# S4 convolution beside a feed-forward block: order of pieces in a spectral visit, six visits for the last inverse step, and a later third bank

## The chip, the core and the metric

The kernel runs on one core of a Trainium2 chip. Its engines run side by side, each through its own list of instructions in order: TensorE (PE, matmuls, with weight loads shown apart as PEld), VectorE (DVE), ScalarE (ACT), GpSimd (POOL) and SyncE (SP, which here only issues transfers). They wait for each other through semaphores. Matmuls write to PSUM, eight banks of 128 partitions x 512 fp32 values; DVE and ACT read the results from there. The metric is the device time of one execution in microseconds, as the median of the runs. In the profile every matmul of fp32 data in small tiles is recorded as two passes; the counts below are of the program's matmuls, unless "recorded" is said.

## The reference

```python
def _A_ref(u, A_re, A_im, B_re, B_im, C_re, C_im, log_dt, Dskip):   # S4 convolution
    dt = jnp.exp(log_dt)[:, None]
    logdA = dt * (A_re + 1j * A_im)
    P = jnp.exp(logdA[:, :, None] * l[None, None, :])               # D x N x L
    K = jnp.einsum("dn,dnl,dn->dl", Cc, P, dt * Bc).real            # kernel of 2048 taps
    y = irfft(rfft(u, 2L) * rfft(K, 2L))[:L] + u * Dskip
    return y
def _B_ref(x, w1, w2):
    return silu(x @ w1) @ w2
xn = layernorm(x)
return x + _A_ref(xn, ...) + _B_ref(xn, w1, w2)
```

(The transform lines are shortened.) L is 2048 tokens, D 576 channels, N 128 states, the hidden width F 4608. All is fp32.

## The kernel before, in words

**The feed-forward block (FFN) is the main stream of PE.** Tokens are worked in halves and blocks of 512, the hidden width in chunks of four tiles of 128. `up()` makes one hidden tile: 14 matmuls of 512 columns into the bank `ph` (lines 343 to 345; each fp32 operand is split into a high and a low part, and three of the four products are kept), then ACT makes `gf` (silu) and its high part `gh`, DVE the low part `gl`. `down()` makes one token tile and half of the channels: a group of twelve matmuls of 288 columns into a bank `po` (line 369), which DVE adds to the accumulator `acc` (line 373). Weights come by DMA and are split by ACT and DVE (`w1h`, `w1l`, `w2h`, `w2l`).

**Banks for `po`.** `banks_of()` (line 114) hands a bank to each group when the program writes it: two banks `ps2` in turn, and every third group the bank `ps3`, whenever `ps3` exists. `ps3` exists while the convolution kernel is generated, not during the spectral stage, and again from the end of that stage (0.876 of the FFN's steps) on. The new `ps3` lies where the spectral stage had its banks.

**The convolution is woven in.** `weave()` steps the FFN generator and moves the generator `side()` on when the FFN has come to a given share of its steps. `side()` first generates the kernel taps, then spreads the input; from 0.601 to 0.876 runs `spectral()`, then `tail()`.

`spectral()` works through 16 pairs of frequencies, each with three kinds of data of 576 columns: the taps `kw` (kind 0), the input `u` (kind 1) and the product `ysw` (kind 2, the first step of the inverse). They are laid end to end and cut into **visits** of up to 1024 columns. `visit()` takes the tile `pf` (pool `psb`, four banks, one buffer: the next visit starts when the banks are evacuated) and issues the visit's pieces, sorted by kind and by descending pair (line 808). A piece is a run of columns of one kind and pair within a bank; it is eight matmuls of 64 x 32 tiles of the array (line 815), which stand side by side in the array. Then ACT and DVE evacuate the pieces in the order in which the visit lists them: `ka` and `ut` by ACT (line 833), `e` by ACT and `yo` by DVE (line 827). DVE makes the products `kb` and `ut` (lines 840 to 844) and the taps `kw` (lines 799 and 801) beside it.

`tail()` does the **last step of the inverse**. `add_conv(j, dsts)` takes four banks `py` (three of `pss`, one of `ps3`) and issues sixteen matmuls of 64 x 32 tiles and 288 columns for the token tiles j and j + 1 (line 947), each bank holding one half of the channels of one tile; DVE adds the four banks to the rows' sums (line 955). There are eight calls: four in `tail()` for tiles 0 to 7, whose sums come back from DRAM as `r0`, and four in `down()` of the last chunk, for tiles 8 to 15, whose sums are still in `acc`.

**What sets the order.** The program's text gives a first order; a scheduler then places the instructions of each engine by its own costs. `high_priority()` moves an instruction up, `behind(x)` forbids it ahead of x. So one moved visit shifts the FFN matmuls around it.

Of the kernel before, what the change touches and what calls it, by code (L numbers as in the profile page):

```python
# [26 lines left out]
HD = D // 2  # L27
# [5 lines left out]
def weave(main, steps, side):  # L33

    at = next(side, None)
    for i, _ in enumerate(main):
        while at is not None and at * steps <= i + 1:
            at = next(side, None)
    while at is not None:
        at = next(side, None)  # L40


@with_exitstack
def kernel(
# [22 lines left out]
    nc = tc.nc  # L67
# [24 lines left out]
    f1 = vt = None  # L92
    s4 = None
# [14 lines left out]
    ps1 = ctx.enter_context(tc.tile_pool(name="ps1", bufs=2, space=PSUM))  # L108
    ps2 = ctx.enter_context(tc.tile_pool(name="ps2", bufs=2, space=PSUM))
    pss = psb = ps3 = None  # L110

    acc = {}

    def banks_of():

        n = 0
        while True:
            n += 1
            pool, tag = (ps3, "ps3") if ps3 and n % 3 == 0 else (ps2, "ps2")
            yield pool.tile([P, 512], F32, tag=tag, name="po")  # L120

    spare = banks_of()

    def new_xt(blk):
# [25 lines left out]
    pins = {}  # L150

    def behind(ins):
        return tc.issue_after(ins) if ins is not None else nullcontext()
# [113 lines left out]
    def ffn():  # L267
# [88 lines left out]
        def down(blk, jj):  # L356
            half, c, b = blk
            j = 8 * half + 4 * b + jj
            js = slice(jj * P, (jj + 1) * P)
            if half == 1 and c == NCH - 1:  # L360
                if jj % 2 == 0:
                    add_conv(j, (acc[j], acc[j + 1]))
            for h in range(2):
                hs = slice(h * HD, (h + 1) * HD)
                po = next(spare)
                n = 0
                for t in range(FT):
                    for g, w in ((0, 0), (0, 1), (1, 0)):
                        pins["pe"] = nc.tensor.matmul(po[:, :HD], G[blk, t][g][:, js], W2[half, c, t][w][:, hs],  # L369
                                                      start=n == 0, stop=n == 3 * FT - 1).ins  # L370
                        n += 1
                with tc.high_priority():
                    nc.vector.tensor_add(acc[j][:, hs], po[:, :HD], acc[j][:, hs])  # L373
# [47 lines left out]
        for i, blk in enumerate(blocks):  # L421
            half, c, b = blk
# [23 lines left out]
            for step in ("u0", "d0", "d1", "d2", "d3", "u1", "u2", "u3"):  # L446
                k = int(step[1])
# [12 lines left out]
    kl = kfp = yp = pa = tail_at = None  # L460
# [293 lines left out]
    def spectral():  # L754
# [49 lines left out]
        def visit(v):  # L804

            banks = psb.tile([P, 2, 2, 512], F32, tag="psb", name="pf")
            last = pins["pe"]
            for kind, p, c, n, b, at in sorted(visits[v], key=lambda piece: (piece[0], -piece[1])):
                for g in (1, 0):
                    gs = slice(64 * g, 64 * g + 64)  # L810
                    for o in (1, 0, 3, 2):
                        os = slice(32 * o, 32 * o + 32)
                        src = (ks[p][gs, 1 - o % 2] if kind == 0 else us[p][gs, o % 2] if kind == 1 else ys[p][gs, o // 2])
                        with tc.high_priority(), behind(last):
                            last = nc.tensor.matmul(banks[os, g, b, at:at + n], mats[p, kind // 2][gs, os], src[:, c:c + n],  # L815
                                                    start=True, stop=True, tile_position=(64 * g, 32 * o),
                                                    skip_group_check=True).ins
            pins["pe"] = last
            for kind, p, c, n, b, at in visits[v]:
                if kind == 2:  # L820
                    if c == 0:
                        yos[p] = kl.tile([P, 2, D], F32, tag="yo", name="yo", bufs=1)
                    e = kl.tile([P, 512], F32, tag="e", name="e", bufs=1)[:, :n]
                    with tc.high_priority():
                        nc.scalar.copy(e, banks[:, 0, b, at:at + n])
                        for h, op in enumerate((ALU.add, ALU.subtract)):
                            pins["turned"] = nc.vector.tensor_tensor(yos[p][:, h, c:c + n], e, banks[:, 1, b, at:at + n], op=op).ins
# [68 lines left out]

    def tail():

        r0s = {}

        def load_r0(j):
            r0s[j] = yp.tile([P, 2, D], F32, tag="r0", name="r0", bufs=4)
            nc.sync.dma_start(r0s[j], dr0[j * P:(j + 2) * P, :].rearrange("(i p) d -> p i d", p=P))

        yield tail_at[0]
        with behind(pins["load"]):
            for j in (0, None, 2, None, None, None, None, None):
                conv_load()
                if j is not None:
                    load_r0(j)  # L910
        for j in range(0, 8, 2):
            if j == 2:
                load_r0(4)
                load_r0(6)
            yield tail_at[1 + j // 4] + j // 2 % 2 * tail_at[3]
            add_conv(j, (r0s[j][:, 0, :], r0s[j][:, 1, :]))
            store(r0s[j], j, (nc.gpsimd,))

    yss = {}

# [14 lines left out]
                nc.sync.dma_start(yss[j][64 * h:64 * h + 64],  # L935
                                  d2.rearrange("(q j r) d -> j r q d", q=4, j=NJ)[j, :, :, h * HD:(h + 1) * HD])

    def add_conv(j, dsts):

        py = [pool.tile([P, 512], F32, tag=t, name="py") for pool, t in ((pss, "pss"),) * 3 + ((ps3, "ps3"),)]  # L940
        first = pins["pe"]
        for n in range(16):
            i, q1, q2, h = 1 - n // 8, n // 4 % 2, n // 2 % 2, 1 - n % 2
            o = 64 * q1 + 32 * q2
            rows = slice(64 * h, 64 * h + 64)
            with tc.high_priority() if n else nullcontext(), behind(first):
                mm = nc.tensor.matmul(py[2 * i + h][o:o + 32, :HD], s4[rows, q2], yss[j + i][rows, 2 * q2 + q1],  # L947
                                      start=True, stop=True, tile_position=(64 * h, o), skip_group_check=True)
            if n == 0:
                first = mm.ins  # L950
        for i in range(2):
            del yss[j + i]
            for h in range(2):
                hs = slice(h * HD, (h + 1) * HD)
                nc.vector.tensor_add(dsts[i][:, hs], py[2 * i + h][:, :HD], dsts[i][:, hs])
        for _ in range(2):
            conv_load()

    def gate_of(i):
# [7 lines left out]
        return t + min(max(t - turn, 0) * lost / (0.5 - turn - lost), lost)  # L967

    def side():
        nonlocal s4, kl, kfp, yp, pa, tail_at, f1, vt, pss, psb, ps3  # L970
        marks = (0.13, 0.601, 0.876)
        tail_at = (0.91, 0.934, 0.967, 0.0072)
        with tc.tile_pool(name="kf", bufs=1) as kfp, tc.tile_pool(name="pss", bufs=3, space=PSUM) as pss, tc.tile_pool(name="ps3", bufs=1, space=PSUM) as ps3:
            for n in ("f", "phi"):
                kf[n] = kfp.tile([P, D], F32, name=n + "T")
            f1 = ident
            vt = kfp.tile([P, 69], F32, name="vt")
# [70 lines left out]
    sd = side()  # L1048
# [97 lines left out]
```

## Time and profile before

| | |
|---|---|
| median of 3 runs | 1092.29 us (1092.09 to 1092.8) |
| profiled execution | 1091.44 us |
| its span | 1089.7 us |
| PE busy | 1080.4 us, 99% |
| DVE busy | 892.1 us, 82% |
| ACT busy | 588.7 us, 54% |
| granted clock of PE | 1.000 |

How to read the rows that follow. A row of the timeline gives the start, the busy time, the engine, the line, the operation, what is written from what, the shape and how many stand in the row; in brackets the time for which the engine was idle before it, and what ended that. PE's matmuls overlap each other in the pipeline, so the spacing of their starts is what one costs, not its busy time. A row of the list of waits gives who waited for whom, the time in all, how often, and the longest. A row of the table by windows gives the window, its length, and for PE and PEld the busy time with the number of recorded instructions, then the clock, the share of DMA and what it moved. A piece of the chain has start, length and what it was.

### The profile page before, as it was taken

What the parts mean: (1) busy time and instruction counts of PE and PEld (TensorE: products, weight loads), DVE (VectorE), ACT (ScalarE), POOL (GpSimd) and SP (SyncE); (2) the same over time, 40 slices, a digit from 0 to 9 for tenths busy, and PEclk for the clock granted to TensorE, in tenths of its full rate; (3) what the DMA queues carried; (4) which work ended last, traced back from release to release, by engine and by line L of the source; (5) the groups of instructions that cost most, each with busy time, mean ns of one, the idle gap of its engine ahead of it and who ended that gap; (6) DMA issues with size and microseconds to landing.
All of it is one profiled execution on the core that took longest, in us unless ns stands there. A gap on an engine that the chain in (4) does not pass through costs nothing.

```text
span 1089.7 us, 24623 instructions
## 1 busy us (share of the span) xinstructions
PE 1080.4 (99%) x10127; PEld 946.9 (87%) x10127; DVE 892.1 (82%) x1463; ACT 588.7 (54%) x934; POOL 138.4 (13%) x241
## 2 busy tenths in 40 slices
PE   9999999999999999999999999999999999999998
PEld 7999998998998999989999898887788787888886
DVE  7799899999999999999999963678888878753443
ACT  4574455767676777676766753435454534432210
POOL 1100000000000000010000004234242432000111
PEclk9999999999999999999999999999999999999999
DMA  9745521342525243427644257558675865438953
GB/s 271 208 125 155 146 67 40 93 113 65 131 70 134 73 102 101 110 82 211 197 133 111 58 119 198 155 152 256 176 226 169 237 179 162 122 99 208 245 159 88
DMA packets 175424, 156.58 MB, mean 144 GB/s; under 512 B 113312, under 2 KB 144800, under 8 KB 175184
## 3 DMA queue, kind: packets, MB, share of 16 engines
q1 hardware_dynamic: 159616, 103.21, 36.8%
q0 software_dynamic: 14944, 50.94, 15.5%
q8 instruction: 79, 1.29, 0.5%
q10 hardware_dynamic: 752, 0.85, 0.3%
q14 instruction: 33, 0.27, 0.1%
HBM read 101.00 MB, written 44.61 MB: 134 GB/s over the span
## 4 chain that ended last, share of the span: by engine, by line
PE 90%; DVE 7%; ACT 1%; issue 1%; DMA 0%; POOL 0%; ACTq 0%; DVEq 0%
PE po L369 40%; PE ph L343 33%; PE pf L815 4%; PE ph L345 3%; PE kp L736 3%; PE ph L344 3%; PE z L663 2%; PE py L947 1%; DVE acc L373 1%; PE pu L171 1%; PE pu L172 1%; DVE gl L354 1%; DVE th L649 1%; DVE S L715 0%; DVE C L704 0%
## 5 line engine op out<-in xcount | busy, mean ns | idle before, releaser
L369 PE MATMUL po<-w2h,gh 128*128 128x288 f32 x1152 | 338.8, 297 | 0.6 <-DVE acc L373 0.6
L369 PE MATMUL po<-w2l,gh 128*128 128x288 f32 x1152 | 339.1, 296 | 0.3 <-DVE w2l L328 0.3
L369 PE MATMUL po<-w2h,gl 128*128 128x288 f32 x1152 | 335.8, 296 | 0.0
L369 PEld LDWEIGHTS po<-w2h,gh 128*128 128x128 f32 x1152 | 215.4, 188 | 16.6 <-issue 6.3
L369 PEld LDWEIGHTS po<-w2l,gh 128*128 128x128 f32 x1152 | 215.8, 188 | 10.4 <-issue 3.8
L369 PEld LDWEIGHTS po<-w2h,gl 128*128 128x128 f32 x1152 | 214.9, 188 | 3.9 <-issue 2.8
L373 DVE TENSOR_TENSOR acc<-po,acc 128x288 f32<-128x288 f32 x288 | 126.2, 452 | 65.9 <-PE po L369 64.8
L351 ACT ACTIVATE gf<-ph 128x512 f32<-128x512 f32 (+1 forms) x146 | 85.3, 587 | 167.2 <-PE ph L345 145.6
L343 PE MATMUL ph<-xh,w1l 128*128 128x512 f32 (+1 forms) x584 | 158.4, 386 | 0.0
L343 PE MATMUL ph<-xh,w1h 128*128 128x512 f32 (+1 forms) x584 | 158.3, 387 | 0.0
L343 PE MATMUL ph<-xl,w1h 128*128 128x512 f32 (+1 forms) x584 | 158.0, 386 | 0.0
L354 DVE TENSOR_TENSOR gl<-gf,gh 128x512 fp32r<-128x512 f32 (+1 forms) x148 | 98.3, 671 | 37.2 <-ACT gh L352 36.3
L343 PEld LDWEIGHTS ph<-xl,w1h 128*128 128x128 f32 x584 | 107.2, 188 | 20.7
L343 PEld LDWEIGHTS ph<-xh,w1l 128*128 128x128 f32 x584 | 107.3, 188 | 20.3
L343 PEld LDWEIGHTS ph<-xh,w1h 128*128 128x128 f32 x584 | 104.0, 188 | 16.8 <-ACT x L143 0.5
L352 ACT CAST gh<-gf 128x512 fp32r<-128x512 f32 (+1 forms) x148 | 89.0, 610 | 51.7 <-PE po L369 49.1
L174 POOL DMA_DIRECT2D d1u<-u x32 | 17.4, 545 | 478.1 <-ACT u L173 478.1
L693 ACT ACTIVATE c<-th,magic 128x1040 f32<-128x1040 f32 x36 | 42.0, 1168 | 39.8 <-DVE C L716 32.0
L695 ACT ACTIVATE c<-th 128x1040 f32<-128x1040 f32 x36 | 38.7, 1075 | 45.6 <-DVE th L694 45.1
L305 DVE TENSOR_TENSOR w1l<-w1r,w1h 128x640 fp32r<-128x640 f32 x72 | 56.5, 818 | 0.2
L345 PE MATMUL ph<-x,w1l 128*128 128x512 f32 (+1 forms) x146 | 56.6, 388 | 0.0
L344 PE MATMUL ph<-x,w1h 128*128 128x512 f32 (+1 forms) x146 | 56.2, 385 | 0.0
(189 smaller groups left out, 1609.7 us busy)
## 6 DMA issues: line engine op xcount, KB each, us to landing
w2r<-in_B_w_dram SPq DMA_DIRECT2D x72, 288.0 KB, 3.7
w1r<-in_B_w_dram SPq DMA_DIRECT2D x35, 512.0 KB, 3.9
d1u<-u POOLq DMA_DIRECT2D x32, 288.0 KB, 2.6
d1k<-stage SPq DMA_DIRECT2D x36, 256.0 KB, 4.7
u<-d1u POOLq DMA_DIRECT2D x16, 576.0 KB, 5.0
kw<-d1k POOLq DMA_DIRECT2D x16, 576.0 KB, 6.0
ysw<-ut SPq DMA_DIRECT2D x64, 144.0 KB, 2.7
d<-yo POOLq DMA_DIRECT2D x32, 288.0 KB, 4.0
```

The lines of the kernel that those rows point to most:

```text
L305: pins["w1l"] = nc.vector.tensor_sub(l1, src, h1).ins
L343: nc.tensor.matmul(ph, w[:, kt, :], v[:, kt, a:e], start=n + kt == 0, stop=False)
L344: nc.tensor.matmul(ph, h1[:, 4, :], x4[:, a:e], start=False, stop=False)
L345: pins["pe"] = nc.tensor.matmul(ph, l1[:, 4, :], x4[:, a:e], start=False, stop=True).ins
L351: nc.scalar.activation(gf, ph, AF.Silu)
L352: pins["gh"] = nc.scalar.copy(gh, gf).ins
L354: pins["gl"] = nc.vector.tensor_sub(gl, gf, gh).ins
L369: pins["pe"] = nc.tensor.matmul(po[:, :HD], G[blk, t][g][:, js], W2[half, c, t][w][:, hs], start=n == 0, stop=n == 3 * FT - 1).ins
L373: nc.vector.tensor_add(acc[j][:, hs], po[:, :HD], acc[j][:, hs])
L693: nc.scalar.activation(c65, th, AF.Identity, bias=magic)
L695: nc.scalar.activation(c65, th, AF.Abs)
L815: last = nc.tensor.matmul(banks[os, g, b, at:at + n], mats[p, kind // 2][gs, os], src[:, c:c + n], start=True, stop=True, tile_position=(6 ...
```

## The change

**Pieces.** A new function `ends_small()` orders the pieces of a visit: of up to three pieces the shortest goes to the front, or stays last if it stood last in the old order; of more than three the two shortest go to the two ends, the one that came earlier in the old order to the front. The rest stay in the old order. Both `visit()` and `add_conv()` use it.

**Last inverse step.** `add_conv(js, dsts)` takes a list of two or three token tiles. With three, the tiles are laid end to end over two banks for each half of the channels: pieces of 288, 224, 64 and 288 columns, each of eight matmuls and two adds. `tail()` does (0, 1, 2), (3, 8, 9), (10, 11, 4) and (5, 6, 7), at 0.934, 0.945, 0.956 and 0.967 of the FFN's steps; `down()` does (12, 13) and (14, 15). The program has 32 matmuls and eight DVE adds more than before. Results of the tiles 0 to 7 are stored once both tiles of a pair are done.

**Third bank.** A flag `third` says whether every third group of `po` goes to `ps3`. It is set at the start of the convolution, cleared before the spectral stage, and set again in `tail()` at 0.91 of the FFN's steps.

```diff
+def ends_small(pieces, key):
+    short = sorted(sorted(pieces, key=lambda piece: piece[3])[:2 if len(pieces) > 3 else 1], key=key)
+    rest = sorted((piece for piece in pieces if piece not in short), key=key)
+    if len(short) == 1 and short[0] == max(pieces, key=key):
+        return rest + short
+    return short[:1] + rest + short[1:]
...
-            pool, tag = (ps3, "ps3") if ps3 and n % 3 == 0 else (ps2, "ps2")
+            pool, tag = (ps3, "ps3") if third and n % 3 == 0 else (ps2, "ps2")
...
             if half == 1 and c == NCH - 1:
-                if jj % 2 == 0:
-                    add_conv(j, (acc[j], acc[j + 1]))
+                if b == 1 and jj % 2 == 0:
+                    add_conv((j, j + 1), acc)
...
-            for kind, p, c, n, b, at in sorted(visits[v], key=lambda piece: (piece[0], -piece[1])):
+            for kind, p, c, n, b, at in ends_small(visits[v], lambda piece: (piece[0], -piece[1])):
...
         yield tail_at[0]
+        third = True
...
-        for j in range(0, 8, 2):
-            if j == 2:
+        for k, js in enumerate(((0, 1, 2), (3, 8, 9), (10, 11, 4), (5, 6, 7))):
+            if k == 1:
                 load_r0(4)
                 load_r0(6)
-            yield tail_at[1 + j // 4] + j // 2 % 2 * tail_at[3]
-            add_conv(j, (r0s[j][:, 0, :], r0s[j][:, 1, :]))
-            store(r0s[j], j, (nc.gpsimd,))
+            yield tail_at[1 + k]
+            add_conv(js, {j: r0s[j - j % 2][:, j % 2, :] if j < 8 else acc[j] for j in js})
+            for j in js:
+                if j < 8 and j % 2:
+                    store(r0s[j - 1], j - 1, (nc.gpsimd,))
...
-    def add_conv(j, dsts):
+    def add_conv(js, dsts):
         py = [pool.tile([P, 512], F32, tag=t, name="py") for pool, t in ((pss, "pss"),) * 3 + ((ps3, "ps3"),)]
...
+        for i, j in enumerate(js):
+            c, at = 0, (512 if len(js) < 3 else HD) * i
+            while c < HD:
+                n = min(HD - c, 512 - (at + c) % 512)
+                pieces.append((i, j, c, n, (at + c) // 512, (at + c) % 512))
+                c += n
...
-        tail_at = (0.91, 0.934, 0.967, 0.0072)
+        tail_at = (0.91,0.934,0.945,0.956,0.967)
...
+            third = True
...
-        ps3 = None
+        third = False
```

**In the order of PE, a pair of visits in the spectral stage** (at 737 us of the profile before). `pf_9005` and `pf_9118` are two visits that follow each other; the second has four pieces. Before, its start and what is around it:

```order
L369 MATMUL po_9345<-w2h_9188,gh_9214 128x288
L815 MATMUL pf_9118<-kw_8767,m2_8765 32x384 x8
L815 MATMUL pf_9118<-u_8763,m2_8609 32x448 x8
L815 MATMUL pf_9118<-u_8763,m2_8609 32x128 x8
L815 MATMUL pf_9118<-ysw_8785,m2_8400 32x64 x8
L369 MATMUL po_9345<-w2l_9189,gh_9214 128x288
```

After:

```order
L379 MATMUL po_9359<-w2h_9188,gh_9214 128x288
L825 MATMUL pf_9118<-u_8763,m2_8609 32x128 x8
L825 MATMUL pf_9118<-kw_8767,m2_8765 32x384 x8
L825 MATMUL pf_9118<-u_8763,m2_8609 32x448 x8
L825 MATMUL pf_9118<-ysw_8785,m2_8400 32x64 x8
L379 MATMUL po_9345<-w2l_9189,gh_9214 128x288
```

The piece of 128 columns has gone to the front. Between the two visits stand 25 FFN matmuls before, 3 of them with 512 columns, and 36 after, 18 of them with 512.

**PE again, at the groups of `po` after the spectral stage** (at 988 us of the profile before). The groups are numbered in the order in which they are handed banks: 12048, 12062, 12076, 12090, 12104, 12118, 12132, 12146. Before, every third of them (12062, 12104, 12146) has the third bank:

```order
L369 MATMUL po_12104<-w2h_11594,gh_11997 128x288
L369 MATMUL po_12104<-w2l_11595,gh_11997 128x288
L369 MATMUL po_12104<-w2h_11594,gl_11998 128x288
L369 MATMUL po_12146<-w2h_11333,gh_11635 128x288
L369 MATMUL po_12146<-w2l_11334,gh_11635 128x288
```

After:

```order
L379 MATMUL po_12132<-w2h_11594,gh_11997 128x288
L379 MATMUL po_12132<-w2l_11595,gh_11997 128x288
L379 MATMUL po_12132<-w2h_11594,gl_11998 128x288
L379 MATMUL po_12146<-w2h_11333,gh_11635 128x288
L379 MATMUL po_12146<-w2l_11334,gh_11635 128x288
```

Before, the two groups that stand side by side have the same bank. After, all of these groups alternate between the two banks of `ps2`, and the group ahead of 12146 has the other bank.

**PE, in the last inverse step** (at 1070 us of the profile before): two calls of `add_conv` with banks `py_12998` to `py_13001` and `py_13089` to `py_13092`. Before:

```order
L947 MATMUL py_12999<-ys_12664,ident_69 32x288
L947 MATMUL py_12998<-ys_12664,ident_69 32x288
L947 MATMUL py_13092<-ys_12825,ident_69 32x288 x4
L947 MATMUL py_13091<-ys_12825,ident_69 32x288 x4
L947 MATMUL py_13090<-ys_12822,ident_69 32x288 x4
```

After, the end of the first of the two calls of two tiles:

```order
L970 MATMUL py_13122<-ys_12738,ident_69 32x288
L970 MATMUL py_13121<-ys_12738,ident_69 32x288 x2
L379 MATMUL po_13145<-w2h_12798,gh_13116 128x288
L379 MATMUL po_13145<-w2l_12799,gh_13116 128x288
L379 MATMUL po_13145<-w2h_12798,gl_13117 128x288
```

Before, two calls follow each other without an FFN matmul between them; after, 42 FFN matmuls stand between this call and the next.

More of the change, by code (lines that the diff above doesn't have):

```diff
@@ L897, in tail @@
     def tail():
+        nonlocal third
         r0s = {}
@@ L936, in conv_load @@
                                   d2.rearrange("(q j r) d -> j r q d", q=4, j=NJ)[j, :, :, h * HD:(h + 1) * HD])
-    def add_conv(j, dsts):
+    def add_conv(js, dsts):
         py = [pool.tile([P, 512], F32, tag=t, name="py") for pool, t in ((pss, "pss"),) * 3 + ((ps3, "ps3"),)]
[L941 to L952, printed above, removed]
+        pieces = []
+        for i, j in enumerate(js):
[4 more added lines that the diff above has]
+                c += n
+        first = last = pins["pe"]
+        for _, j, c, n, b, at in ends_small([(i, j, c, n, b, at) for i, j, c, n, b, at in pieces], lambda piece: -piece[4]):
+            for q in range(4):
+                for h in (1, 0):
+                    q1, q2 = q // 2, q % 2
+                    o = 64 * q1 + 32 * q2
+                    rows = slice(64 * h, 64 * h + 64)
+                    with nullcontext() if first is last else tc.high_priority(), behind(first):
+                        mm = nc.tensor.matmul(py[2 * b + h][o:o + 32, at:at + n], s4[rows, q2], yss[j][rows, 2 * q2 + q1, c:c + n],
+                                              start=True, stop=True, tile_position=(64 * h, o), skip_group_check=True)
+                    if first is last:
+                        first = mm.ins
+        for _, j, c, n, b, at in pieces:
+            yss.pop(j, None)
@@ L953, in add_conv @@
             for h in range(2):
-                hs = slice(h * HD, (h + 1) * HD)
-                nc.vector.tensor_add(dsts[i][:, hs], py[2 * i + h][:, :HD], dsts[i][:, hs])
-        for _ in range(2):
+                d = dsts[j][:, h * HD + c:h * HD + c + n]
+                nc.vector.tensor_add(d, py[2 * b + h][:, at:at + n], d)
+        for _ in js:
             conv_load()
@@ L969, in side @@
     def side():
-        nonlocal s4, kl, kfp, yp, pa, tail_at, f1, vt, pss, psb, ps3
+        nonlocal third, s4, kl, kfp, yp, pa, tail_at, f1, vt, pss, psb, ps3
         marks = (0.13, 0.601, 0.876)
-        tail_at = (0.91, 0.934, 0.967, 0.0072)
+        tail_at = (0.91,0.934,0.945,0.956,0.967)
         with tc.tile_pool(name="kf", bufs=1) as kfp, tc.tile_pool(name="pss", bufs=3, space=PSUM) as pss, tc.tile_pool(name="ps3", bufs=1, space=PSUM) as ps3:
+            third = True
             for n in ("f", "phi"):
@@ L1037, in side @@
         nc.gpsimd.dma_start(s4, cs4)
-        ps3 = None
+        third = False
         with tc.tile_pool(name="kl", bufs=2) as kl, tc.tile_pool(name="psb", bufs=1, space=PSUM) as psb:
```

## The prediction

> **What bounds the kernel now.** I read the page first, then the list of waits of the matrix engine, then its timeline around each wait, then the chain through those places, and last the busy time of single visits.
>
> ```profile
> span 1089.7 us, 24623 instructions
> PE 1080.4 (99%) x10127; PEld 946.9 (87%) x10127; DVE 892.1 (82%) x1463; ACT 588.7 (54%) x934; POOL 138.4 (13%) x241
> PE 90%; DVE 7%; ACT 1%; issue 1%; DMA 0%; POOL 0%; ACTq 0%; DVEq 0%
> ```
>
> The matrix engine (PE) is busy 99% of the span and is 90% of the chain that ended last. So a microsecond is won or lost only where PE stands still, or where its matmuls take longer than the same columns take elsewhere. The profiled execution took 1091.44 us, its span is 1089.7, and it stands 0.85 below the median of 1092.29; I make the sum against 1091.44 and add 0.85 at the end. 0.2% of the median, about what a measurement of this kernel can tell from no change, is 2.18 us: the bounds are 1090.1 and 1094.5.
>
> The list of PE's waits from 676 us on has four rows:
>
> ```profile
> PE py L947 <- DVE r L955: 0.6, 1, 0.6
> PE po L369 <- DVE acc L373: 0.6, 1, 0.6
> PE pf L815 <- issue: 0.4, 1, 0.4
> PE po L369 <- DVE w2l L328: 0.3, 1, 0.3
> ```
>
> Each is a single event, 1.9 us in all, and all of them lie in the stretch that the change rewrites. The holes around them are larger than the list says, because it counts only time in which no matmul is running, and after each stop the pipeline has to fill again. So I measure from start to start.
>
> **The change part by part. (a) The wait of a visit at 737 us.** PE's timeline and three pieces of the chain before it:
>
> ```profile
> 736.61 0.29 PE L369 MATMUL po<-w2h,gh 128*128 128x288 f32 x1
> 737.36 0.88 PE L815 MATMUL pf<-kw,m 64*32 64x384 f32 x16 [0.45 <-issue]
> ...
> 739.52 0.29 PE L369 MATMUL po<-w2h,gl 128*128 128x288 f32 x1
> 739.66 0.29 PE L369 MATMUL po<-w2h,gh 128*128 128x288 f32 x1
> 740.22 0.40 PE L369 MATMUL po<-w2l,gh 128*128 128x288 f32 x1 [0.27 <-DVE w2l L328]
> 740.45 0.30 PE L369 MATMUL po<-w2h,gl 128*128 128x288 f32 x1
> 740.59 0.29 PE L369 MATMUL po<-w2h,gh 128*128 128x288 f32 x1
> 740.88 0.40 PE L369 MATMUL po<-w2l,gh 128*128 128x288 f32 x1
> ```
> ```profile
> 726.60 0.46 DVE acc L373
> ...
> 736.57 0.39 DVE yo L827
> ...
> 739.49 0.68 DVE w2l L328
> ```
> For comparison an undisturbed visit:
> ```profile
> 860.51 0.29 PE L369 MATMUL po<-w2h,gh 128*128 128x288 f32 x1
> 860.73 1.20 PE L815 MATMUL pf<-kw,m 64*32 64x64 f32 x32
> ...
> 862.62 0.40 PE L369 MATMUL po<-w2l,gh 128*128 128x288 f32 x1
> ```
>
> Undisturbed, a visit starts 0.22 us after the FFN matmul ahead of it (860.51 to 860.73), and an FFN matmul of 288 columns follows the last one after 0.14 (739.52 to 739.66). At 737 the visit starts 0.75 after: 0.53 lost. 739.66 to 740.22 is 0.56, so 0.42 lost, and 740.59 to 740.88 0.29, so 0.15. After each of these two stops the next start comes 0.23 instead of 0.14 later (740.22 to 740.45): 0.2 together. The sum is 1.3 us. The cause is one: from 726.60, when PE delivers the sum `po_9076`, VectorE (DVE) works without a pause until 740.17 (739.49 plus 0.68), and the evacuation `yo` of the visit before, which the visit needs because the four banks exist once, is in that row at 736.57, and `w2l` behind it.
>
> In the new order 36 FFN matmuls stand between the two visits in place of 25, and 18 of them are 512 wide in place of 3. DVE has the same nineteen operations between `po_9076`'s sum and the second `w2l` in both orders, so they still take 13.6 us (726.60 to 740.17). The eleven more matmuls alone, at 0.14 each, give PE 1.5 us more work before it needs either result, against 0.53 that are lacking at the visit and 0.42 more at `w2l`. These matmuls are no extra work; PE does them later in the order of before. So (a) is worth -1.3; bounds: -1.3 if all goes, -0.5 if only the visit's own wait goes, since 1.5 less 0.95 leaves a cover of only half a microsecond.
>
> **(b) The third bank at 988 us.**
>
> ```profile
> 987.83 0.29 PE L369 MATMUL po<-w2h,gl 128*128 128x288 f32 x1
> 988.68 0.40 PE L369 MATMUL po<-w2h,gh 128*128 128x288 f32 x1 [0.55 <-DVE acc L373]
> ...
> 990.25 0.29 PE L369 MATMUL po<-w2h,gl 128*128 128x288 f32 x1
> 990.49 0.99 PE L369 MATMUL po<-w2h,gh 128*128 128x288 f32 x3
> 991.32 0.30 PE L369 MATMUL po<-w2l,gh 128*128 128x288 f32 x1
> ...
> 991.59 0.29 PE L369 MATMUL po<-w2h,gh 128*128 128x288 f32 x1
> 991.82 0.40 PE L369 MATMUL po<-w2l,gh 128*128 128x288 f32 x1
> ```
>
> `po_12104` ends at 987.83 and `po_12146` follows directly; both were handed the third bank, so the second waits for the whole chain matmul, `acc` add, matmul. By starts: 987.83 to 988.68 is 0.85, 0.71 too much; the restart 0.09, as at 740.22; then the stop has delayed the release of the buffers of `gh`, and 990.25 to 990.49 loses 0.10, 990.49 to 991.32 (three matmuls, due 0.42) loses 0.41, 991.59 to 991.82 and the restart behind it 0.09 each. Sum 1.5 us. With the third bank handed out from 0.91 on only, these groups alternate between two banks, with twelve matmuls of another group between a bank's end and its next use: 12 x 0.14 = 1.7 us against the 0.85 that bank and add took here. What is late next is the first use of the third bank, `po_12372`; it stands well behind the last evacuation. I take -1.5; bounds -1.5 and 0 (the holes at 990 to 992 come back in another place if `gh` has another holder).
>
> **(c) The order of pieces in a visit.** Busy time of PE in visits of 1024 columns, the last row of two answers of the table by windows: nine visits in which a short piece stands behind a long one with another behind it, and the seventeen others.
>
> ```profile
> sum 25.90, PE 18.72 PEld 9.18; mean PE 2.08 PEld 1.02
> ```
> ```profile
> sum 50.10, PE 33.23 PEld 15.05; mean PE 1.95 PEld 0.89
> ```
>
> All have the same columns; nine of them cost 18.72 - 9 x 1.95 = 1.2 us more. The visit at 860.73 has its 64 columns first and takes 1.89 from its start to the next FFN matmul, so a short piece at the front costs nothing; others of the seventeen have it last. The new rule puts the short ones there in every visit, so I take -1.1 (1.2 less 0.1 for pieces that the scheduler may still mix). Bounds: -1.2, and +0.4 if visits now undisturbed become like the mean of the nine in three cases (3 x 0.13). The loads of `u` and `kw` that change places in the queues of GpSimd and SP cost nothing: no DMA is in the list of waits; their cover is the second buffer of each of these tiles, and without it a late load would show as a wait of `pf`, at a price like that of (a).
>
> The rule also makes one visit fall apart: its piece `u` of 256 columns is issued eleven FFN matmuls ahead of the rest. **A visit's fixed cost** comes from two sizes. The first add_conv:
>
> ```profile
> 1012.74 1.23 PE L947 MATMUL py<-ys,ident 64*32 64x288 f32 x32
> 1013.90 0.41 PE L369 MATMUL po<-w2h,gh 128*128 128x288 f32 x1
> ```
>
> 576 columns take 1.16, 1024 take 1.89: (1.89 - 1.16) / 448 = 1.63 ns a column and 0.22 fixed. Around it lie 0.22 - 0.14 ahead and 0.23 - 0.14 behind, so 0.39 us for each further visit. The split costs +0.4.
>
> **(d) The last step of the inverse.** Eight calls of two tiles become four of three tiles and two of two. Two of the eight stand side by side today:
>
> ```profile
> 1070.55 1.22 PE L947 MATMUL py<-ys,ident 64*32 64x288 f32 x32
> 1072.34 1.78 PE L947 MATMUL py<-ys,ident 64*32 64x288 f32 x32 [0.57 <-DVE r L955]
> 1074.06 0.40 PE L369 MATMUL po<-w2h,gh 128*128 128x288 f32 x1
> ```
> ```profile
> 1071.83 1.55 DVE L955 TENSOR_TENSOR r<-py,r 128x288 f32<-128x288 f32 x4 [2.92 <-PE py L947]
> ```
>
> This pair takes 3.51, where 2 x 1.16 would do: its second half waits for the banks and then goes at the pace of DVE's adds. Before: 6 x 1.16 + 3.51 + 7 x 0.17 around them = 11.7. After: a visit of three tiles has 864 columns, 1.16 + 288 x 1.63 ns = 1.63; 4 x 1.63 + 2 x 1.16 + 6 x 0.17 = 9.9. That is -1.8; the pair stands 42 FFN matmuls apart now. But in the new order the pieces of a three-tile visit stand mixed, and by the nine visits above that costs 0.13 each at most places: I allow 0.1 x 4, so -1.4. Bounds -1.8, and -0.4 (0.22 each, as the dearest of the nine, and one wait of 0.57 for a bank). The 32 more matmuls are in the columns already: a visit of 1024 columns costs the same in 32 recorded passes as in 64.
>
> ```profile
> 730.50:733.40 2.90, 1.95 (x32) 0.49 (x32) 1.00 0.02 6
> ...
> 788.40:791.40 3.00, 1.96 (x64) 1.11 (x64) 1.00 1.06 255
> ```
>
> Against this stands a rule of the Trainium skill, "TensorEngine Tiling (Array Packing)", section Instruction Overhead: each matmul has an overhead of about 60 cycles, so one should not cut a dimension that is small already. If that came on top, eight more matmuls a visit, side by side on eight tiles, would be two passes of 60 cycles; at 0.8 ns a column and pass (half of 1.63) I estimate 0.1 us a visit, 0.4 in all, and the sum would be 0.4 higher. The two rows above speak for nothing on top.
>
>  The eight more adds (by 1.55 / 4 = 0.39 each, 3 us) lie beside PE's work; without that cover they are the second rival. The stores of tiles 4 to 7 move behind the last call; they leave well ahead of the last rows, which are unchanged.
>
> **The sum.** -1.3 - 1.5 - 1.1 + 0.4 - 1.4 = -4.9. For waits that a new order of some 3000 matmuls makes where the trace of before can show none I add +0.4, one wait like that at 740.22. -4.5 on 1091.44 gives 1086.9, and with 0.85, 1087.8 as the median.
>
> **The rivals.** First, the waits move and do not go. (a) and (b) are lateness of DVE and of `gh`, and an order that saves PE 1 us brings it 1 us earlier to the next late result. Against it: outside these places no DVE wait is in the list, and between them PE is the late one. Then -1.1 + 0.4 - 1.4 is left, -2.1: 1090.2, within 0.2%.
>
> Second, DVE paces the three-tile visits. Each leaves eight adds, 3.1 us by the row of 1071.83, and the four banks exist once; between the second and the third such visit stand only 18 FFN matmuls of 512 columns, 0.23 us each by these two rows, 4.2 us:
>
> ```profile
> 1029.73 1.09 PE L343 MATMUL ph<-xh,w1h 128*128 128x512 f32 x4
> 1030.66 1.08 PE L343 MATMUL ph<-xl,w1h 128*128 128x512 f32 x4
> ```
>
> If a `gl` (0.69 in the chain) and two other adds come between, the third waits as at 1072.34, and (d) gives 0.57 and the slow half back: 3.51 - 2 x 1.16 = 1.2. The time is 1089.0.
>
> Third, order within a visit does not matter and the dear nine have another cause. The Trainium skill, "TensorE: Matmul & The Clock Gate", Part 3, gives the span of a pack of tiles as the duration of one matmul and about 4 ns for each further tile, with no term for the order of unlike sizes; by that rule -1.1 is 0. As a mechanism here: the nine are slow because of the weight loads or data that stand there, and keep 2.08. The time is 1088.9. Against it: same columns, same engines, and the two groups differ in order only.
>
> Fourth, slower: the four banks of `pf` become the bound. ACT and DVE evacuate in the old order of pieces whatever order they were issued in, so an evacuation can wait for a piece that now comes last, and the next visit waits for it. Its price is that of (a), 1.3 us each. Without (a), the other terms make -3.6; it takes five of the 26 distances between visits to come to +2.9, 1095.2, and four leave it within 0.2%. Against it: one of 26 waited before, and the distances are alike.
>
> **How the numbers follow.** The forecast with its terms: 0.62, within 1086.4 to 1088.8. First rival 0.13 (half of it beyond 1090.1), second 0.08, third 0.11, fourth 0.06. Faster by over 0.2%: 0.62 + 0.08 + 0.11 and a little of the first, 0.84; within: 0.10; slower: 0.06. The low end is all terms at their bound: -1.3 - 1.5 - 1.2 + 0.4 - 1.8 = -5.4, so 1086.9 by the sum, and 0.5 less for what small holes I did not list: 1086.4. The high end reaches the first rival, 1090.3.
>
> **What would show it.** In the profile after: no wait of `pf` near 737 and none of `po` on `acc` near 988; busy time of PE in every visit of 1024 columns 1.95 to 1.97; six pieces of `py`, those of three tiles about 1.65 from start to the next FFN matmul, and no wait of `py` on DVE. Wrong it is if the list of waits has new rows of over a microsecond, most likely `pf` for a bank between 700 and 760 or `py` for an add.

## The result and the profile after

| | before | after |
|---|---|---|
| median of ten runs | 1091.99 us | 1089.09 us |
| range | 1091.23 to 1092.93 | 1087.94 to 1089.81 |
| profiled execution | 1091.44 us | 1089.77 us |
| its span | 1089.7 us | 1087.9 us |

The ratio is 0.9973, 95% interval 0.9963 to 0.9983: 2.9 us faster, where 4.5 was forecast. The page after:

```profile
span 1087.9 us, 24745 instructions
PE 1080.2 (99%) x10191; PEld 948.6 (87%) x10191; DVE 891.6 (82%) x1471; ACT 589.2 (54%) x934; POOL 138.2 (13%) x241
PE 85%; DVE 8%; DMA 3%; issue 2%; ACT 2%; SPq 1%; DVEq 0%; ACTq 0%
```

PE is still the bound, but the chain now runs through a transfer (DMA 3%, against 0% before). The list of PE's waits from 676 us on has one row left, with a name that the four rows before did not have:

```profile
PE pf L825 <- DMA ysw<-ut: 0.6, 2, 0.4
```

All four old waits are gone; a new one stands at two places. The timeline at both:

```profile
852.99 0.74 PE L825 MATMUL pf<-kw,m 64*32 64x320 f32 x16
853.92 1.31 PE L825 MATMUL pf<-ysw,m 64*32 64x384 f32 x32 [0.18 <-DMA ysw<-ut]
...
901.89 0.85 PE L825 MATMUL pf<-kw,m 64*32 64x384 f32 x16
903.11 1.33 PE L825 MATMUL pf<-ysw,m 64*32 64x448 f32 x32 [0.37 <-DMA ysw<-ut]
```

From the start of `kw` to that of `ysw` pass 0.93 and 1.22 us. At 1.63 ns a column 320 and 384 columns are due after 0.52 and 0.63, so 0.41 and 0.59 us are lost there. With the disturbed passes behind them it is more: PE's busy time in the two visits by windows is

```profile
sum 8.00, PE 4.62 PEld 2.55; mean PE 2.31 PEld 1.27
```

where 2 x 1.95 would do. That is 0.7 us too much, and with the idle 0.18 and 0.37 it makes 1.3.

The place at 737 us after: five FFN matmuls, the visit, and twelve more follow each other in the chain, without a wait between:

```profile
737.75 0.66 PE po L379 x5
738.41 1.89 PE pf L825 x64
740.30 1.79 PE po L379 x12
```

The table by windows over the 23 visits of 1024 columns that wait for nothing, its last row (23 x 1.95 = 44.9), and the six pieces of the last inverse step, with the four of three tiles first:

```profile
sum 68.50, PE 44.96 PEld 20.11; mean PE 1.95 PEld 0.87
```
```profile
1008.90:1012.00 3.10, 2.02 (x64) 1.25 (x64) 1.00 1.09 244
1033.00:1036.00 3.00, 2.12 (x64) 1.34 (x64) 1.00 0.00 0
1039.40:1042.60 3.20, 2.36 (x64) 1.71 (x64) 1.00 1.05 301
1050.30:1053.40 3.10, 1.94 (x64) 1.22 (x64) 1.00 0.36 82
```
```profile
sum 18.50, PE 10.98 PEld 6.85; mean PE 1.83 PEld 1.14
```

The same sum before, over its seven pieces:

```profile
sum 23.60, PE 10.43 PEld 4.72; mean PE 1.49 PEld 0.67
```

So the spectral visits are as clean as forecast, but the three-tile visits, due at 1.63 and some 0.06 for the last pass, are at 1.94 to 2.36.

One thing about comparing two single traces. PE's order is the same in both kernels up to the first visit, and yet it starts at another time:

```profile
681.47 1.20 PE L815 MATMUL pf<-kw,m 64*32 64x512 f32 x32
```
```profile
682.29 1.20 PE L825 MATMUL pf<-kw,m 64*32 64x64 f32 x32
```

0.8 us of the spans' difference is no effect of the change. From the first visit to the end it is 408.2 us before (1089.7 - 681.47) and 405.6 after: 2.6 us less, near the 2.9 of the medians. I account from there.

### The profile page after: what moved, and what is told of

It reads as the page before. It is cut to its first block, busy times and chain, and to the rows that moved or that the text cites. A ratio compares the mean times of both kernels' runs of the same rounds, so it can differ in the third digit from the quotient of the medians.

```text
span 1087.9 us, 24745 instructions
## 1 busy us (share of the span) xinstructions
PE 1080.2 (99%) x10191; PEld 948.6 (87%) x10191; DVE 891.6 (82%) x1471; ACT 589.2 (54%) x934; POOL 138.2 (13%) x241
## 4 chain that ended last, share of the span: by engine, by line
PE 85%; DVE 8%; DMA 3%; issue 2%; ACT 2%; SPq 1%; DVEq 0%; ACTq 0%
PE po L379 37%; PE ph L353 32%; PE pf L825 4%; PE ph L354 3%; PE ph L355 3%; PE kp L746 2%; PE z L673 1%; DMA ysw<-ut 1%; PE py L970 1%; DVE acc L383 1%; DMA acc<-in_A_u_dram 1%; DVE th L659 1%; DVE gl L364 1%; DVE S L725 1%; PE pu L181 1%
```

## Experiments

Every experiment was run beside the kernel before on the same chip, 5 to 11 times. "Against the changed kernel" is the difference of two ratios, at 1092 us. An interval reaches 1 to 1.7 us to either side. Of the runs that keep most of the change, only the combination of both remedies at the end and the two slow runs have an interval clear of the changed kernel's 0.9963 to 0.9983; for the others the difference in time is an indication, and the traces have to say what it is made of.

**One part at a time.** Only the order of pieces:

```diff
-            for kind, p, c, n, b, at in sorted(visits[v], key=lambda piece: (piece[0], -piece[1])):
+            for kind, p, c, n, b, at in ends_small(visits[v], lambda piece: (piece[0], -piece[1])):
```

> Only the order of pieces in a spectral visit is taken over; banks and the last inverse step are as before. If the new order itself makes the two waits for `ysw` near 852 and 901 us, they show here too (0.5 and 0.7 us), the nine dear visits fall by 0.13 each, the wait at 737 is gone or not by where the scheduler puts the visits: the time is 0.3 to 1.3 us under the kernel before. If the waits came from another part of the change, no `pf` waits for `ysw` and the time is 2 us under it or more.

Measured: 1091.47 us, ratio 0.9993 (0.9984 to 1.0002), 0.8 us, which the interval doesn't tell from nothing. Its waits:

```profile
PE po L378 <- DVE acc L382: 1.1, 2, 0.6
PE py L956 <- DVE r L964: 0.6, 1, 0.6
PE pf L824 <- DMA ysw<-ut: 0.5, 1, 0.5
```

The wait at 737 and the one for `w2l` are gone by the order alone. `ysw` is waited for by the order alone too. Seven of the nine visits that were dear before (the two others are those that wait for `ysw`) are at the price of the rest, by the last row of the windows:

```profile
sum 21.00, PE 13.69 PEld 6.36; mean PE 1.96 PEld 0.91
```

A second group of `po` now waits for `acc`, which it did not before. Both waits, of 0.55 us each, lie at the place of the third bank, at 986.74 and 989.13 us.

Only the third bank:

```diff
-            pool, tag = (ps3, "ps3") if ps3 and n % 3 == 0 else (ps2, "ps2")
+            pool, tag = (ps3, "ps3") if third and n % 3 == 0 else (ps2, "ps2")
...
         yield tail_at[0]
+        third = True
```

> Only the third bank is handed out later. Theory: the wait of 0.55 us at 988 and the holes after it are gone and nothing else changes: 1.5 us faster than the kernel before. Rival, the lateness moves on to the next user of `gh` or of a bank: 0 to 0.3 us, with a wait of another name between 960 and 1010.

Measured: 1089.85 us, ratio 0.9980 (0.9971 to 0.9989), 2.2 us faster, more than either theory said. Its waits are those of 737, and no others:

```profile
PE pf L816 <- issue: 0.4, 1, 0.4
PE po L370 <- DVE w2l L329: 0.3, 1, 0.3
```

The wait at 988 is gone as expected. The rest is that of `py` for `r`: with the banks dealt otherwise, the scheduler no longer puts two calls of the last inverse step side by side, and eight separate calls cost PE

```profile
sum 27.10, PE 10.10 PEld 4.77; mean PE 1.26 PEld 0.60
```

against 10.43 in seven pieces and a wait of 0.57.

Only the six visits of the last inverse step (the changed kernel with the two other parts undone):

> Only the six visits of the last inverse step. Theory from the trace of the changed kernel: the three-tile visits take 1.9 to 2.3 us each instead of 1.63 because their matmuls are mixed, so the gain against the kernel before is only 0.3 us and the place at 988 still waits. The prediction's term was 1.4 us.

Measured: 1092.21 us, ratio 1.0000 (0.9991 to 1.0008). Nothing is gained, and the waits at 988 and 737 are there as before:

```profile
PE po L379 <- DVE acc L383: 0.5, 1, 0.5
PE pf L825 <- issue: 0.4, 1, 0.4
PE po L379 <- DVE w2l L338: 0.3, 1, 0.3
```

The three alone give 0.8 + 2.2 + 0.0 = 3.0 us, together 2.9. That they add up so well is partly luck, since they are not independent: the order alone brings a second wait at 988, which the third bank removes, and the third bank alone parts two calls, which the six visits would have parted too.

**The last inverse step undone in the changed kernel**, so eight calls of two tiles with the new order of pieces and the new dealing of banks:

> The changed kernel with the last inverse step as before, eight calls of two tiles. In the run with the third bank alone these eight did not merge and cost 11.6 us with what is around them, against 12.2 for the six of the changed kernel. Theory: the six visits bring nothing, and without them the time is 0 to 0.6 us under the changed kernel. Rival (the prediction's): the six are worth over a microsecond and the time is 1 us or more above it.

Measured: 1088.32 us, ratio 0.9963 (0.9952 to 0.9975). Against the changed kernel it is 1.1 us faster, by intervals that overlap; it is not slower, as the prediction's term of 1.4 would have it. The calls do not merge here either: 10.10 us of PE in eight pieces. Not all of the 1.1 us belongs to the calls. In this trace the spectral visits stand in the order of the changed kernel, but the visit at 901 us does not wait for `ysw` (1.89 us to the next FFN matmul against 2.62). From the last spectral visit to the end the eight calls are 0.7 us faster than the six.

**Why three-tile visits are dear.** The changed kernel, with each matmul of a call held behind the one before it:

```diff
-        first = last = pins["pe"]
+        first, last = None, pins["pe"]
...
-                    with nullcontext() if first is last else tc.high_priority(), behind(first):
+                    with nullcontext() if first is None else tc.high_priority(), behind(last):
...
-                    if first is last:
-                        first = mm.ins
+                    first = last = mm.ins
```

> The changed kernel, with each matmul of the last inverse step held behind the one before it, so that the eight tiles of a piece stand together. Theory (the mixing is what makes the three-tile visits dear): they take 1.6 to 1.7 us from the first start to the next FFN matmul, 1.5 us less in sum, and the kernel is 1.2 to 1.8 us faster than the changed one. Rival (the cut into pieces of unlike size, or the four banks, make them dear): they stay at 1.9 to 2.3 us and the time does not move.

Measured: 1088.27 us, ratio 0.9961 (0.9949 to 0.9974), 1.3 us faster than the changed kernel. The last three of the three-tile visits by windows:

```profile
1033.00:1036.00 3.00, 1.69 (x64) 0.93 (x64) 1.00 0.11 18
1037.30:1040.30 3.00, 1.69 (x64) 0.93 (x64) 1.00 1.07 241
1049.30:1052.30 3.00, 1.69 (x64) 0.93 (x64) 1.00 0.32 71
```

All are alike at 1.69, against 2.12, 2.36 and 1.94, with the same pieces in the same banks. The mixing is what made them dear, not the cut into unlike pieces nor the banks. The first visit, though, comes a little earlier and meets a wait that the later start had hidden:

```profile
1007.88 0.34 PE L970 MATMUL py<-ys,ident 64*32 64x64 f32 x16
1009.59 1.58 PE L970 MATMUL py<-ys,ident 64*32 64x288 f32 x48 [1.37 <-DMA ys<-d]
```

This stop takes what the calls give: from the first visit to the end the trace is no shorter than that of the changed kernel (405.8 and 405.6 us), and the 1.3 us are those of the five runs. So the same with the first call one FFN step later, `tail_at = (0.91, 0.937, ...)`:

> The changed kernel with the matmuls of the last inverse step held in order and its first call one FFN step later. Theory: the wait of 1.4 us for `ys` that the held order alone met is gone, the six calls cost 10.4 us, the waits for `ysw` stay: 1.8 us faster than the changed kernel, about 1087. Rival: a call further back waits instead, no gain over the held order alone (1088.3).

Measured: 1087.21 us, ratio 0.9955 (0.9942 to 0.9967), 2.0 us faster than the changed kernel, near the expected 1.8, with no wait of `py`. Part of it is luck in the traced run: both waits for `ysw` were expected to stay, and the one at 901 is missing.

**Where the wait for `ysw` comes from.** First an attempt by the order of pieces:

```diff
+    if len(short) == 2 and short[1][0] == 2 and rest[-1][0] == 2:
+        return short + rest
     return short[:1] + rest + short[1:]
```

> The changed kernel, but where the rule would put the short piece of the older `ysw` last and so the newer `ysw` ahead of it, both short pieces go to the front and the newer `ysw` is issued last, 0.2 to 0.3 us later within the visit. Theory (the two waits at 852 and 901 us come from the newer product being wanted earlier): they shrink by 0.3 each or vanish, 0.6 to 1.2 us faster than the changed kernel. Rival (the transfer itself lands later in the new order, whatever the place in the visit): the waits stay, the time does not move.

Measured: 1096.58 us, ratio 1.0037 (1.0025 to 1.0049), 7 us slower than the changed kernel. The expectation rested on a mistake: the two pieces of `ysw` in these visits (384 and 192, 448 and 128, each 576 in sum) are one tile, cut at a bank, and not an older and a newer one. The edit therefore wanted the same transfer earlier, and the wait grew:

```profile
PE py L972 <- DMA ys<-d: 3.7, 2, 1.9
PE pf L827 <- DMA ysw<-ut: 2.2, 2, 1.6
```

As the changed kernel wants `ysw` no earlier within these visits than the old order did (behind the other two pieces in both), the theory that the place in the visit made the wait is gone too. The larger loss is the other row. The spectral visits near the end fall differently (the last but one is in two parts in both kernels: here at 947.98 and 954.57, in the changed kernel at 946.58 and 950.56), the last inverse step is loaded later (its first load is issued at 998.4 in place of 991.7), and its first call, whose place is fixed by the FFN's steps, stands and waits:

```profile
1010.14 0.81 PE L972 MATMUL py<-ys,ident 64*32 64x64 f32 x20 [1.93 <-DMA ys<-d]
1012.74 3.08 PE L972 MATMUL py<-ys,ident 64*32 64x288 f32 x44 [1.80 <-DMA ys<-d]
```

The stop costs more than its 3.7 us. The rows of the call by windows show a granted clock of 0.52 for what follows the second stop; in the run with the held order, where PE stood still for 1.37 us, it stayed at 1.00:

```profile
1012.70:1015.80 3.10, 3.06 (x44) 1.51 (x44) 0.52 1.09 231
```
```profile
1009.50:1011.30 1.80, 1.58 (x48) 0.84 (x48) 1.00 1.09 229
```

The same order of pieces with the held matmuls and the later first call:

> The changed kernel with three things together: the matmuls of the last inverse step held in order, the older `ysw` first, and the first call of the last inverse step one step of the FFN later (0.937 for 0.934). Theory: no wait of `py` for `ys` (1.4 us in the run with the order alone), no or small waits for `ysw`, three-tile visits at 1.63 us; 2.5 to 3.2 us faster than the changed kernel, about 1086. Rival: the first call comes too late for the ones behind it, or another transfer is late, and it is not better than the run with the held order alone, about 1088.3.

Measured: 1089.00 us, ratio 0.9971 (0.9960 to 0.9983), 0.2 us faster than the changed kernel in place of the expected 2.5 to 3.2. `py` no longer waits, and the six calls cost what they should; the two waits for `ysw`, 2.4 us in the list, take it back.

Then the transfer itself. In the old order the four quarters of `ysw` at 892 us, which the visit at 900 needs, are issued by SP in 2.67 us, and GpSimd issues the load of `u` behind them; in the changed kernel the load falls together with the last quarter. SP's and GpSimd's issues before:

```profile
892.17 2.67 SPq L848 DMA_DIRECT2D ysw<-ut  x4
```
```profile
894.93 0.71 POOL L781 DMA_DIRECT2D u<-d1u  x1 [7.24 <-PE pf L815]
```

and after, where the four take 3.78 us:

```profile
894.38 3.78 SPq L858 DMA_DIRECT2D ysw<-ut  x4
```
```profile
896.51 0.72 POOL L791 DMA_DIRECT2D u<-d1u  x1 [6.54 <-PE pf L825]
```

The last quarter, from issue to landing in us (the last figure), before and after:

```profile
ysw<-ut SPq DMA_DIRECT2D x1, 144.0 KB, 3.7
```
```profile
ysw<-ut SPq DMA_DIRECT2D x1, 144.0 KB, 6.5
```

At 845 us, for the visit at 852, this account does not hold. There the load of `u` stood beside the quarters in the old order too, and SP issued them in 2.44 us:

```profile
844.83 2.44 SPq L848 DMA_DIRECT2D ysw<-ut  x4
```
```profile
844.89 0.71 POOL L781 DMA_DIRECT2D u<-d1u  x1 [7.06 <-PE pf L815]
```

The last quarter there landed after 5.5 us before and 6.1 after. In the old order it was in time by only 0.2 us (issued at 846.68, wanted at 852.37), so half a microsecond is enough for a wait. Why it is slower in the new order is not shown.

The experiment puts the load of `u` on SP, behind the quarters; PE's order of visits stays:

```diff
-                nc.gpsimd.dma_start(us[p], uv[p])
+                (nc.sync if p > 1 else nc.gpsimd).dma_start(us[p], uv[p])
...
-                    load_u(p + 2)
                     load_m(p + 3, 0)
...
                     for _ in products(p):
                         pass
+                    load_u(p + 2)
```

> The changed kernel, with the load of `u` of a later pair issued by SP behind the four transfers of `ysw` instead of by GpSimd beside them; PE's order of visits stays word for word. Theory (the last quarter of `ysw` lands late because it shares the DMA engines with the load of `u`, which in the new order starts with it): `ysw` lands within 4 us of its issue near 847 and 896 us, the two waits go, 0.9 to 1.3 us faster than the changed kernel. Rival (DVE makes the product late, the transfer is not the point): the waits stay at 0.4 to 0.7 us.

Measured: 1087.46 us, ratio 0.9956 (0.9942 to 0.9970), 1.9 us faster than the changed kernel by the ratios, more than the expected 0.9 to 1.3. The intervals overlap, but every run (1086.91 to 1087.60) is below every run of the changed kernel (1087.94 to 1089.81). The list of PE's waits from 676 us on is empty. The issues at the same place, and the last quarter:

```profile
893.69 2.41 SPq L858 DMA_DIRECT2D ysw<-ut  x4
896.20 1.24 SPq L791 DMA_DIRECT2D u<-d1u  x1
ysw<-ut SPq DMA_DIRECT2D x1, 144.0 KB, 4.0
```

It lands after 4.0 us here, as expected, but after 5.8 at 847, where under 4 was expected; the 0.3 us less than the 6.1 suffice. At 901 the first quarter is issued 8.1 to 8.2 us ahead of the due start of `ysw` with and without this edit, so it is not DVE's product that came late here (in the kernel before it was 8.6 us, so the new order takes 0.4 us of slack). By the two traces the visits at 852 and 901 take 1.96 and 1.89 us to the next FFN matmul in place of 2.41 and 2.62, 1.2 us less together. The rest of the spans' difference of 2.1 lies where nothing was changed, 0.2 ahead of the first visit and 0.7 behind the last matmul.

How late `ysw` is differs between traces with the same order of visits and `u` on GpSimd. At 852 it starts late in all five (changed kernel, order alone, held order, later first call, eight calls), by 0.4 to 0.8 us; at 901 it is late by 0.6, 0.3 and 0.2 in the first three and in time in the last two. With `u` behind it on SP it starts as due at both places, here and in the next run.

Both together, this and the held and later calls:

> The two before together: the sum of their gains, 2.7 to 3.1 us faster than the changed kernel, about 1086. If a transfer on SP now delays the weights, a wait of PE or of ACT for `w1` or `w2` between 690 and 960 us takes some of it back.

Measured: 1086.02 us (1085.23 to 1087.03), ratio 0.9945 (0.9933 to 0.9958): 6.1 us faster than the kernel before and 3.1 faster than the changed one, the fastest of the study. Its list of waits from 676 us on is empty as well, and the six calls cost PE 9.16 us:

```profile
sum 19.00, PE 9.16 PEld 4.69; mean PE 1.53 PEld 0.78
```

**Whether the ends matter.** The changed kernel with every visit's pieces by rising length:

> The changed kernel with the pieces of every spectral visit issued by rising length instead of short ones at both ends. If a short piece is dear only when it stands behind a longer one with another behind it, all visits of 1024 columns without a wait stay at 1.95 us of PE's busy time. If it needs the long ones in the middle, visits with several short pieces in front cost 0.05 to 0.2 us more.

Measured: 1096.41 us, ratio 1.0041 (1.0025 to 1.0057). The largest part of the loss is again at the first call of the last inverse step, since the last visits come late: `py` waits 2.7 us for `ys`, the granted clock is 0.50 behind it, and the call takes 6.6 us to the next FFN matmul in place of 1.95. `pf` also waits, three times, 2.1 us in all. But four visits that wait for nothing show the price that was asked for, one with pieces of 64, 448 and 512 columns and three of 64, 128, 384 and 448. The first two of them:

```profile
778.00:781.00 3.00, 2.08 (x48) 0.99 (x48) 1.00 0.61 222
832.50:835.50 3.00, 2.07 (x64) 1.15 (x64) 1.00 0.17 22
```

In the changed kernel the first of these, as 64, 512, 448, is among the 1.95. So a short piece at the front is not enough to be free, and "a short piece behind a long one with another behind it" does not tell which sequences are dear. What does stays open.

## Why the prediction was right, and where it was not

The direction is right, and the median of 1089.09 lies within the whole range. It lies above the 1086.4 to 1088.8 that the forecast gave to its own terms. The range reached further only for the first rival, whose mechanism did not come: the waits at 737 and 988 are gone. So the number is near, and two of the steps behind it failed.

- **(a) The wait at 737.** Right: the rows at 738 show no stop, and the run with the order alone lost both rows, `pf` and `w2l`. The worth of 1.3 is read off the trace before; no run has this wait alone removed, so its size is not measured. The second wait for `acc` in that run lies at 988 and is gone with the third bank.
- **(b) The third bank.** Right at its place: with this part alone no `po` waits for `acc`. The part is worth 2.2 us by itself, because it also parts the two merged calls of the last inverse step. The prediction had booked that gain under (d).
- **(c) The order of pieces.** Right in size: 23 undisturbed visits at 1.95 of busy time. The split visit is there as well. The third rival is refuted: seven of the nine visits fell from 2.08 to 1.96 with the order alone changed. The rule of the Trainium skill's "TensorE: Matmul & The Clock Gate", Part 3, has no term for the order; here the same visits differ by 0.12 us with the order alone. The reason that the prediction gave, "a short piece at the front costs nothing", is not right in general, by the run with rising lengths.
- **(d) The last inverse step.** Here a term was mis-sized: -1.4 was forecast; PE's busy time in these calls rose from 10.43 to 10.98 and only the wait of 0.57 and one transition were saved, and with this part alone the time did not move. The step that failed is "I allow 0.1 x 4" for the mixed pieces. By the windows it was 2.02, 2.12, 2.36 and 1.94 against the 1.69 of the held order, 1.7 us in sum. The price had been taken from spectral visits, in which each matmul is held behind the one before it, so that the eight tiles of a piece stand together; here matmuls of different pieces were mixed. The second rival, DVE's adds, did not come: no wait of `py` for DVE is in the list. Against eight calls that do not merge, the six were 0.7 us slower.
- **The queues.** The step that failed outright is "the loads of `u` and `kw` that change places ... cost nothing", with the second buffer as cover. The buffer covers `u`, but not the transfer that `u` runs beside: `ysw` was in time by 0.2 us at 852 before. Its wait cost 1.3 us at the two places in the profiled run, and the traces with `u` issued behind `ysw` have neither. The remedy shows that the load of `u` is what delays `ysw`; it does not separate the moment of the load from its queue. The size differs from run to run, and why `ysw` lands later at 852 in the new order is not explained.
- **The sum.** From the first visit on: -1.3 - 1.5 - 1.1 + 0.4 as forecast, -0.2 in place of -1.4 for (d) (10.98 - 10.43 - 0.57 - 0.17), and +1.3 for `ysw` in place of the +0.4 that stood for the unknown. That makes -2.4, and the two traces have -2.6. The agreement is partly luck, as the +1.3 is that of one traced run.

## What to carry to other kernels

A reordering of the bottleneck engine also shifts when transfers are released, so look at the transfers with the least slack and what now starts beside them, not only at those that move. A stop of PE can cost more than its idle time, so look at the granted clock behind it. When small matmuls share the array, pin the order in which their tiles are issued: left to a scheduler, the same columns cost up to 40% more (2.36 against 1.69). And before cutting work into fewer pieces, test whether the expensive pair can just be kept apart, which another part of this change did for nothing.

## What had not been expected of the hardware

- Four transfers of 144 KB took SP 2.67 us to issue with GpSimd's load of `u` behind them, 3.78 with it beside the last of them, and 2.44 with it beside the first; with `u` behind them on SP, 2.41.
- After stops of 1.93 and 1.80 us with 20 recorded matmuls between them, the granted clock of PE was 0.52 over the next 44 (older `ysw` first); after single stops of 1.37 us (held order) and 1.57 us (older `ysw` first, at 904) it stayed at 1.00.
- Mixed order within a pack of 64 x 32 tiles: 1.94 to 2.36 us of PE's busy time for 864 columns, 1.69 in order, with the same number of matmuls.
- A single trace's start-up can differ by 0.8 us in a part of the program that is the same (681.47 and 682.29), a third of the whole effect here.
